# A gated mix of multi-query attention and a state-space convolution: the last softmax normalisation on TensorE, the skip term moved to the end, wide copies for the masters, and four merged stores

## The chip, the cores and the metric

The kernel runs on one core of a Trainium2 chip. The metric is the device time of one execution in microseconds; the span of a profile, from first to last instruction, is about 1.8 us shorter than the time of the same run (552.4 against 554.21 us for the profile of the kernel before).

Engines are named as in the profile: PE multiplies matrices (PEld are its weight loads) and leaves the sums in the memory called PSUM, DVE is the vector engine, ACT the scalar engine, POOL is GpSimd, and SPq and ACTq mark DMA transfers issued by SP and by ACT. To evacuate a tile is to copy it out of PSUM.

## The reference

Two branches read the same x (2048 tokens by 448 channels) and are mixed by a gate per token. Cut to what matters:

```python
g = sigmoid((x * gate_w).sum(-1, keepdims=True))
# A: attention, 16 query heads of 28, one key and value head
q = (x @ wq).reshape(B, S, 16, 28);  k = x @ wk;  v = x @ wv
p = softmax(einsum("bhqd,bkd->bhqk", q, k) * 28 ** -0.5)
a = einsum("bhqk,bkd->bhqd", p, v).reshape(B, S, 448) @ wo
# B: diagonal state space model with 256 states per channel, as a causal convolution
K = einsum("dn,dnl,dn->dl", C, exp(dt * A * l), dt * B).real
b = causal_conv(x, K) + x * Dskip
return g * a + (1 - g) * b
```

## The kernel before

One program for all engines is built from a list of operations with priorities (a smaller number goes first). A list scheduler, which knows an estimated duration for each, fixes the order on every engine before the kernel runs. Four streams share the core:

- Attention. 1024 score tiles (matmul of q and k into PSUM), an exponential on ACT over two or three tiles at once, a value matmul that accumulates in one PSUM bank. The keys' ones column makes row 28 of each group of 32 the softmax denominator. After 16 key tiles the sum is normalised, and after four head groups it is projected with `wo`.
- Tables on the DVE. For each of 28 chunks of 16 channels, powers of the discrete state matrix are doubled up from "masters". Kernel generation on PE turns a table into the convolution kernel, which is evacuated and written to DRAM (`KP_scratch`).
- The convolution on PE: for each chunk four groups of 32 matmuls, each group on one 1 MB Toeplitz tile T that a DMA reads from `KP_scratch` into one of four slots. Then a scaling by 1 - g (`cst`), a transposition on PE (`ytr`) and an add into O, which touches every row of O.
- The skip term x * Dskip * (1 - g), and the stores.

The parts that the change and the argument touch, shortened to a sketch (cuts are marked with `...`):

```python
def norm(self, qc, g):                       # normalisation of head group i = 4 * qc + g
    pg.op("dve", tensor_copy(acc[a], psB))                         # sums out of PSUM
    pg.dma(denT[a] <- row 28 of each 32 of acc[a])                 # (1) spread over 128 partitions
    pg.op("dve", reciprocal(denT[a]))
    pg.dma(R_scratch[i] <- denT[a])                                # (2) to DRAM
    pg.dma(rdenB <- R_scratch[i], each row broadcast to 32 partitions)   # (3) four DMAs
    pg.op("dve", tensor_tensor(onT[i], acc[a], rdenB, MULT))
...
def skip(self):                              # early, priority 53; O was loaded with x before
    for i in range(16):
        pg.op("dve", scalar_tensor_tensor(O[i], O[i], 1 - g, Dskip, MULT, MULT))
...
def masters(self, b):                        # for each of 11 powers k of 7 blocks
    ...
    pg.op("dve", tensor_copy(mbf.real, mst.real))                  # 128 fp32 -> bf16
    pg.op("dve", tensor_tensor(mbf.imag_pair, mst.imag twice, sgn, MULT))   # 256, both signs
...
def kgen(self, c): ... pg.op("pe", mm, pr=3)          # kernel generation
def ytr(self, c):  ... pg.op("pe", mm, pr=3.5)        # transposition of the convolution result
def store(self, i): pg.dma(out[128 rows of i] <- O[i])          # i = 0..15, one queue
```

The DRAM arrays, PSUM banks and the schedule are in the full listing.

Of the kernel before, what the change touches and what calls it, by code (L numbers as in the profile page):

```python
# [11 lines left out]
P = 128  # L12
# [41 lines left out]
class Prog:  # L54
# [13 lines left out]
    def op(self, eng, fn, ns, rd=(), wr=(), pr=0, lat=60, lock=None, unlock=None, comm=None, slack=None, mode="full"):  # L68
        o = Op()
        if eng == "dve" and lat == 60:  # L70
            lat = 105
        o.i, o.eng, o.fn, o.ns, o.lat, o.pr = len(self.ops), eng, fn, ns, lat, pr
        o.lock, o.unlock, o.slot, o.ndma = lock, unlock, None, 0
        o.comm, o.mode = comm, mode
        o.slack = slack if slack is not None else (self.SLACK.get(eng, 0.0) if pr >= 2 else 0.0)
        deps = {}
        if comm is not None:
            deps[self.lastw[comm]] = 1
            self.commops.setdefault(comm, []).append(o.i)
        for k in rd:  # L80
            for c in self.commops.get(k, ()):
                deps[c] = 1
            w = self.lastw.get(k)
            if w is not None:
                deps[w] = 1
        for k in wr:
            w = self.lastw.get(k)
            if w is not None:
                deps[w] = 1
            for r in self.readers.get(k, ()):  # L90
                deps.setdefault(r, 0)
        for k in rd:
            self.readers.setdefault(k, []).append(o.i)
        for k in wr:
            self.lastw[k] = o.i
            self.readers[k] = []
        deps.pop(o.i, None)
        o.deps = deps
        self.ops.append(o)
        return o  # L100
# [15 lines left out]
    def schedule(self):  # L116
# [20 lines left out]
        while done < n:  # L137
            best = None
            for e in ENG:
                T = free[e]  # L140
                for i in ready[e]:
# [7 lines left out]
                    if o.comm in comm:  # L149
                        r = max(r, ops[comm[o.comm]].end)  # L150
# [13 lines left out]
            if o.comm is not None:  # L164
                if o.comm in comm:
                    o.deps[comm[o.comm]] = 1
                comm[o.comm] = i
# [127 lines left out]
class Kernel:  # L295
# [10 lines left out]
    def build(self):  # L306
        nc = self.nc
        with self.es:
# [8 lines left out]
            self.oload()  # L317
# [7 lines left out]
    def alloc(self):  # L325
# [24 lines left out]
        self.dskb = sb("dskb", D, BF)  # L350
# [12 lines left out]
        self.LV = 192  # L363
        self.MC = 5 * 192 + 96
# [5 lines left out]
        self.sgn = sb("sgn", 8, F32)  # L370
# [12 lines left out]
    def consts(self):  # L383
# [10 lines left out]
        for c, val in enumerate([-1.0, 1.0, 1.0, -1.0]):  # L394
            pg.op("pool", lambda e, c=c, val=val: e.memset(V(self.sgn, c, 1), val), 60, wr=["sgn"])
# [18 lines left out]
    def loads(self):  # L414
# [33 lines left out]
        pg.dma([(self.dskb.v(0, P, 0, [[1, D]]), dram(ins["B_Dskip"], 0, [[0, P], [1, D]]))], (128, 896), "dsk", wr=["dsk"])  # L448
# [7 lines left out]
    def oload(self):  # L456
        pg = self.pg
        x = self.ins["A_x"]
        pg.dma([(self.O.v(0, P, 0, [[D, 16], [1, D]]), dram(x, 0, [[D, P], [P * D, 16], [1, D]]))],
               (2048, 896), "ox", rd=[("kT", 3)], wr=["O"], pr=4)  # L460

    def skip(self):
        pg = self.pg
        for i in range(16):
            ov = self.O.v(0, P, D * i, [[1, D]])
            pg.op("dve", lambda e, ov=ov, i=i: e.scalar_tensor_tensor(ov, ov, self.gtok.v(0, P, 16 + i, [[1, 1]]),
                                                                      self.dskb.v(0, P, 0, [[1, D]]), ALU.mult, ALU.mult),
                  el(D), rd=["gt", "dsk", "O"], wr=[("o", i)], pr=53)
        pg.op("dve", lambda e: e.tensor_copy(self.gb.v(0, P, 0, [[1, 16]]), self.gtok.v(0, P, 16, [[1, 16]])), 90,
              rd=["gt"] + [("o", i) for i in range(16)], wr=["O"], pr=53)  # L470
# [5 lines left out]
    def uload(self):  # L476
        pg, x = self.pg, self.ins["A_x"]
        pg.dma([(bass.AP(tensor=self.U.h, offset=16 * D, ap=[[2 * self.U.rs, 64], [1024, 7], [1, 1024]]),
                 dram(self.Z, 0, [[0, 64], [0, 7], [1, 1024]]))], (448, 2048), "uz", rd=["pad", "sw"], wr=["U"], pr=2)
        rs = self.U.rs  # L480
# [87 lines left out]
    def seeds(self):  # L568
# [30 lines left out]
        for s in range(2):  # L599
            o = s * 8192 + 4096 + 31 * 4  # L600
            w = [("tab", s, 0)] + [("xst", k) for k in range(4)] + [("raw", k) for k in range(5)]
            for comp in range(2):
                pg.op("dve", lambda e, o=o, comp=comp: e.memset(self.tab.v(0, P, o + 128 * comp, [[256, 8], [1, 4]]), 1.0 - comp), 80, wr=w, pr=1.5)
# [86 lines left out]
    def masters(self, b):  # L690
# [4 lines left out]
        mo = (b % 2) * self.BC * MC  # L695
        pr = 51.5 + c0 if b else 1.4
# [12 lines left out]
        def src3(k, comp):  # L709
            base = self.seedz if k == 0 else mst  # L710
            off = comp * W2 + B0 if k == 0 else (k % 2) * 2 * BW + comp * BW
            return base.v(0, P, off, [[HC, BC], [1, HC]])

        def src4(k):
            base = self.seedz if k == 0 else mst
            off = W2 + B0 if k == 0 else (k % 2) * 2 * BW + BW
            return base.v(0, P, off, [[4, 8 * BC], [0, 2], [1, 4]])
        for k in range(11):
            ks = "sz" if k == 0 else ("ms", k % 2)
            if k < 5:  # L720
                ro, io, sg = k * 192, k * 192 + 64, 0
            elif k == 5:
                ro, io, sg = 5 * 192, 5 * 192 + 32, 0
            else:
                ro, io, sg = (k - 6) * 192 + 32, (k - 6) * 192 + 128, 2
            lk = ("mb", b % 2, k)
            if k:
# [10 lines left out]
            pg.op("dve", lambda e, k=k, ro=ro: e.tensor_copy(mbf.v(0, P, mo + ro, [[MC, BC], [1, HC]]), src3(k, 0)),  # L738
                  el(BW, 1.92), rd=kk, wr=[lk], pr=pr)
            pg.op("dve", lambda e, k=k, io=io, sg=sg: e.tensor_tensor(  # L740
                mbf.v(0, P, mo + io, [[MC, BC], [1, 64]]), src4(k),
                self.sgn.v(0, P, sg, [[0, 8 * BC], [1, 2], [0, 4]]), ALU.mult),
                el(2 * BW), rd=kk + ["sgn"], wr=[(lk, 1)], pr=pr)

    def tables(self, c):
# [3 lines left out]
        qp = to + 4096  # L749
        b = max(i for i, (c0, n) in enumerate(self.blocks) if c0 <= c)  # L750
        ci = c - self.blocks[b][0]
        mo = (b % 2) * self.BC * self.MC + ci * self.MC
# [4 lines left out]
        pg.op("dve", lambda e: e.tensor_copy(tab.v(0, P, qp + 2048 + 31 * 4, [[256, 8], [128, 2], [1, 4]]),  # L757
                                             self.seedw.v(0, P, c * HC, [[4, 8], [W2, 2], [1, 4]])),
              110, rd=["sw"], wr=[("tab", s, 0)], pr=pr)
        for lv in range(5):  # L760
            w = 1 << lv
            m = mo + lv * 192
# [3 lines left out]
            so_, do_ = qp + (32 - w) * 4, qp + (32 - 2 * w) * 4  # L766
            src = tab.v(0, P, so_, [[128, 32], [1, 4 * w]])
            dst = tab.v(0, P, do_, [[128, 32], [1, 4 * w]])
            pg.op("dve", lambda e, d=dst, a=src, m=m, w=w: e.tensor_tensor(  # L769
                d, a, mbf.v(0, P, m, [[4, 16], [0, 2 * w], [1, 4]]), ALU.mult),  # L770
                el(n, 1.92), rd=rk + mk, wr=[("tab", s, lv + 1)], pr=pr)
            pg.op("dve", lambda e, a=src, m=m, w=w: e.tensor_tensor(  # L772
                tmp.v(0, P, so, [[4 * w, 32], [1, 4 * w]]), a,
                mbf.v(0, P, m + 64, [[4, 32], [0, w], [1, 4]]), ALU.mult),
                el(n, 1.92), rd=rk + mk, wr=[("tmp", s)], pr=pr)
            d2 = tab.v(0, P, do_, [[256, 16], [128, 2], [1, 4 * w]])
            t2 = tmp.v(0, P, so + 4 * w, [[8 * w, 16], [-4 * w, 2], [1, 4 * w]])
            pg.op("dve", lambda e, d=d2, t=t2: e.tensor_tensor(d, d, t, ALU.add), el(n, 1.92),  # L778
                  rd=[("tmp", s), ("tab", s, lv + 1)], wr=[("tab", s, lv + 1)], pr=pr)
        m = mo + 5 * 192  # L780
        mk = [("mb", b % 2, 5), (("mb", b % 2, 5), 1)]
        rk = [("tab", s, l) for l in range(6)]
        src = tab.v(0, P, qp, [[1, 2048]])
        ua = tab.v(0, P, to, [[1, 2048]])
        ub = tab.v(0, P, to + 2048 + 128, [[256, 8], [-128, 2], [1, 128]])
        pg.op("dve", lambda e: e.tensor_tensor(ua, src, mbf.v(0, P, m, [[4, 8], [0, 64], [1, 4]]), ALU.mult),  # L786
              el(2048, 1.92), rd=rk + mk, wr=[("tab", s, 6)], pr=pr)
        pg.op("dve", lambda e: e.tensor_tensor(ub, src, mbf.v(0, P, m + 32, [[4, 16], [0, 32], [1, 4]]), ALU.mult),  # L788
              el(2048, 1.92), rd=rk + mk, wr=[("tab", s, 7)], pr=pr)

    def kgen(self, c):
# [3 lines left out]
        qp = to + 4096  # L795
        tab = self.tab
        X = ("kx", c)
        for jj, comp in ((jj, comp) for jj in range(4) for comp in range(2)):
            def mm(e, jj=jj, comp=comp):
                for half in range(2):  # L800
                    for g in range(4):
                        o = (4 * half + g) * 256 + comp * 128 + jj
                        r = e.matmul(  # L803
                            self.psX.v(32 * g, 32, 96 * jj, [[1, 96]]),
                            tab.v(0, P, qp + 2048 + o, [[4, 32]]), tab.v(0, P, to + o, [[2048, 3], [4, 32]]),
# [3 lines left out]
            pg.op("pe", mm, 165, rd=[("tab", s, l) for l in range(8)], wr=[X, ("kst", c % 2)], pr=3, mode="c32",  # L809
# [23 lines left out]
    def ytr(self, c):  # L833
# [4 lines left out]
        def mm(e):  # L838
            for k in range(4):
# [7 lines left out]
        pg.op("pe", mm, 375, rd=[("cst", cs), "id"], wr=[X], pr=3.5, lock="X", mode="c64")  # L847
        ov = self.O.v(0, P, 15 * D + 16 * c, [[-D, 16], [1, 16]])
        pg.op("dve", lambda e: e.tensor_tensor(ov, ov, self.psX.v(0, P, 0, [[1, 16], [16, 16]]), ALU.add),  # L849
              el(256), rd=[X], comm="O", pr=2, unlock="X")  # L850
# [27 lines left out]
    def outp(self, qc, tt, bank):  # L878
# [3 lines left out]
        lock = "X" if bank == 7 else None  # L882
        kb = [] if bank == 7 else [("b", bank)]
        for g in range(4):
            pg.op("pe", lambda e, g=g: e.matmul(t.v(0, P, o, [[1, D]]), self.onT.v(0, P, ((4 * qc + g) % 6) * 512 + 128 * tt, [[1, 128]]),  # L885
                                                self.Wo.v(0, P, g * D, [[1, D]]), start=(g == 0), stop=(g == 3),
                                                tile_position=(0, 0), skip_group_check=True), 190,
                  rd=["Wo"] + [("on", (4 * qc + k) % 6) for k in range(4)], wr=[X] + kb, pr=2, lock=lock if g == 0 else None)
# [3 lines left out]
              el(D), rd=[X, "gt"] + kb, comm="O", pr=2, unlock=lock)  # L892

    def store(self, i):
        self.pg.dma([(dram(self.out, i * P * D, [[D, P], [1, D]]), self.O.v(0, P, D * i, [[1, D]]))],
                    (128, 896), f"out{i}", rd=["O"], pr=1)

    def norm(self, qc, g):
        pg = self.pg
        i = qc * 4 + g  # L900
        a = i % 2
# [4 lines left out]
        far = 0 if i == 15 else 5000  # L906
# [11 lines left out]
    def main(self):  # L918
# [46 lines left out]
        self.skip()  # L965
# [43 lines left out]
        while c < NCH + LAG:  # L1009
            chunk_step(c)  # L1010
            c += 1
        for tt in range(4):
            self.outp(3, tt, tt)
        for i in range(16):
            self.store(i)
# [48 lines left out]
```

## Time and profile before

| | before |
|---|---|
| time, median | 555.26 us (552.48 to 558.66, 4 runs) |
| span of the profile | 552.4 us |
| last exponential ends | 514.4 us |
| last kernel evacuation starts | 502.7 us |
| last projection add ends | 540.9 us |
| last convolution add ends | 542.9 us |

### The profile page before, as it was taken

To read this page: it belongs to the slowest core of one execution; us is meant where nothing else is said; L and a number is where in the kernel's file an instruction comes from. 1 tells how busy PE (TensorE), PEld (TensorE's weight loads), DVE (VectorE), ACT (ScalarE), POOL (GpSimd) and SP (SyncE) were. 2 spreads that over 40 slices of the span, in tenths; PEclk is the share of its full clock that TensorE was granted. 3 is DMA by queue.
4 is the path that set the end of the run, shared out by engine and by line. 5 is a ranking of instruction groups with operands and counts; after the bars stand their busy time and mean duration, and the time that the engine had idled before them with its cause. 6 is when DMAs were issued, how large, how long until landed. Compare 5 with 4: busy or idle time off the path is not lost.

```text
span 552.4 us, 18386 instructions
## 1 busy us (share of the span) xinstructions
PE 483.9 (88%) x8213; PEld 243.9 (44%) x8213; DVE 489.1 (89%) x1146; ACT 486.7 (88%) x428; POOL 4.7 (1%) x19
## 2 busy tenths in 40 slices
PE   6768978998998999999999999898999999899652
PEld 5411122453544434545455354454554455445421
DVE  3978999999999999999999999999999999991211
ACT  4599999999999999999999999999999999999200
POOL 3000000000000000000000000000000000000000
PEclk9765565999999999999999999999999999989957
DMA  8905408488587378878967786779988798778934
GB/s 227 222 2 133 135 26 305 168 299 332 176 305 289 108 291 298 311 266 305 310 222 257 269 283 199 281 273 369 309 266 316 263 321 309 248 263 288 363 150 133
DMA packets 42014, 136.60 MB, mean 247 GB/s; under 512 B 8684, under 2 KB 24992, under 8 KB 27600
## 3 DMA queue, kind: packets, MB, share of 16 engines
q1 hardware_dynamic: 41200, 135.07, 71.0%
q8 instruction: 64, 1.05, 0.7%
q10 hardware_dynamic: 736, 0.37, 0.3%
q14 instruction: 14, 0.11, 0.1%
HBM read 131.43 MB, written 3.86 MB: 245 GB/s over the span
## 4 chain that ended last, share of the span: by engine, by line
PE 40%; DVE 30%; ACT 21%; DMA 5%; POOL 1%; issue 1%; SPq 0%; POOLq 0%
ACT expT L948 20%; PE psS L938 12%; PE psS L864 10%; PE psB L956 7%; DVE tmp L772 5%; DVE tab L769 5%; DVE tab L778 4%; PE psX L803 4%; DMA T<-KP_scratch 3%; DVE tab L786 2%; PE psX L885 2%; DVE tab L788 2%; DMA R_scratch<-denT 2%; DVE mbf L740 1%; PE psX L678 1%; PE psS L506 1%
## 5 line engine op out<-in xcount | busy, mean ns | idle before, releaser
L948 ACT ACTIVATE expT<-psS 128x1536 bf16<-128x1536 f32 (+1 forms) x410 | 470.0, 1252 | 14.2 <-PE psB L956 9.6
L938 PE MATMUL psS<-qT,kT 29*128 29x512 bf16 x1024 | 172.2, 416 | 34.0 <-ACT expT L948 32.2
L864 PE MATMUL psS<-T,U 128*32 128x128 bf16 (+7 forms) x3584 | 157.4, 303 | 7.2 <-DMA T<-KP_scratch 7.2
L864 PEld LDWEIGHTS psS<-T,U 128*32 128x32 bf16 (+7 forms) x3584 | 113.5, 152 | 39.8 <-issue 24.7
L956 PE MATMUL psB<-expT,vaug 128*32 128x512 bf16 x1024 | 109.7, 419 | 2.4 <-ACT gtok L645 1.4
L938 PEld LDWEIGHTS psS<-qT,kT 29*128 29x128 bf16 x1024 | 39.6, 92 | 130.5 <-ACT expT L948 101.4
L769 DVE TENSOR_TENSOR tab<-tab,mbf 128x1024 bf16<-128x1024 bf16 (+4 forms) x140 | 79.2, 568 | 0.4
L778 DVE TENSOR_TENSOR tab<-tab,tmp 128x1024 bf16<-128x1024 bf16 (+4 forms) x140 | 79.1, 569 | 0.5
L772 DVE TENSOR_TENSOR tmp<-tab,mbf 128x1024 bf16<-128x1024 bf16 (+4 forms) x140 | 79.2, 569 | 0.0
L803 PE MATMUL psX<-tab 128*32 128x96 bf16 x1792 | 58.3, 269 | 1.0 <-DVE O L849 0.8
L956 PEld LDWEIGHTS psB<-expT,vaug 128*32 128x32 bf16 x1024 | 26.7, 95 | 66.6 <-issue 62.2
L803 PEld LDWEIGHTS psX<-tab 128*32 128x32 bf16 x1792 | 43.9, 116 | 12.4 <-issue 6.0
L786 DVE TENSOR_TENSOR tab<-tab,mbf 128x2048 bf16<-128x2048 bf16 x28 | 34.2, 1222 | 0.0
L788 DVE TENSOR_TENSOR tab<-tab,mbf 128x2048 bf16<-128x2048 bf16 x28 | 34.1, 1219 | 0.0
L872 DVE TENSOR_TENSOR cst<-psS,omq 128x512 bf16<-128x512 f32 x28 | 19.2, 685 | 13.9 <-PE psS L864 13.9
L740 DVE TENSOR_TENSOR mbf<-mst,sgn 128x256 bf16<-128x256 f32 x70 | 29.6, 423 | 0.0
L728 DVE TENSOR_TENSOR msq<-mst 128x256 f32<-128x256 f32 x63 | 26.6, 422 | 0.0
L678 PE MATMUL psX<-xT,Wq 112*128 112x512 bf16 x64 | 21.2, 428 | 0.9 <-DVE kstg L818 0.8
L731 DVE TENSOR_TENSOR mst<-msq 128x128 f32<-128x128 f32 x70 | 20.2, 289 | 0.0
L915 DVE TENSOR_TENSOR onT<-acc,rdenB 128x512 bf16<-128x512 f32 x16 | 11.0, 688 | 9.9 <-DMA rdenB<-R_scratch 9.9
L734 DVE SCALAR_TENSOR_TENSOR mst<-mst 128x128 f32<-128x128 f32 x63 | 18.3, 290 | 0.0
L738 DVE CAST mbf<-mst 128x128 bf16<-128x128 f32 x70 | 15.8, 225 | 0.0
(103 smaller groups left out, 248.6 us busy)
## 6 DMA issues: line engine op xcount, KB each, us to landing
T<-KP_scratch SPq DMA_DIRECT2D x112, 1024.0 KB, 8.0
rdenB<-R_scratch SPq DMA_DIRECT2D x64, 64.0 KB, 4.1
U<-in_A_x_dram SPq DMA_DIRECT2D x3, 896.0 KB, 5.4
tab<-in_A_x_dram SPq DMA_DIRECT2D x4, 448.0 KB, 6.9
O<-in_A_x_dram SPq DMA_DIRECT2D x1, 1792.0 KB, 9.9
KP_scratch<-kstg SPq DMA_DIRECT2D x28, 64.0 KB
out_dram<-O SPq DMA_DIRECT2D x16, 112.0 KB, 1.8
U<-Z_scratch SPq DMA_DIRECT2D x1, 896.0 KB, 7.9
```

The lines of the kernel that those rows point to most:

```text
L678: pg.op("pe", lambda e, T=T: e.matmul(px, self.Wq.v(0, DT, T * 512 + g * 128, [[1, 128]]), self.xT.v(0, DT, T * S + 512 * qc, [[1, 512]]), ...
L740: pg.op("dve", lambda e, k=k, io=io, sg=sg: e.tensor_tensor(mbf.v(0, P, mo + io, [[MC, BC], [1, 64]]), src4(k), self.sgn.v(0, P, sg, [[0, ...
L769: pg.op("dve", lambda e, d=dst, a=src, m=m, w=w: e.tensor_tensor(d, a, mbf.v(0, P, m, [[4, 16], [0, 2 * w], [1, 4]]), ALU.mult), el(n, 1.9 ...
L772: pg.op("dve", lambda e, a=src, m=m, w=w: e.tensor_tensor(tmp.v(0, P, so, [[4 * w, 32], [1, 4 * w]]), a, mbf.v(0, P, m + 64, [[4, 32], [0, ...
L778: pg.op("dve", lambda e, d=d2, t=t2: e.tensor_tensor(d, d, t, ALU.add), el(n, 1.92), rd=[("tmp", s), ("tab", s, lv + 1)], wr=[("tab", s, l ...
L786: pg.op("dve", lambda e: e.tensor_tensor(ua, src, mbf.v(0, P, m, [[4, 8], [0, 64], [1, 4]]), ALU.mult), el(2048, 1.92), rd=rk + mk, wr=[(" ...
L788: pg.op("dve", lambda e: e.tensor_tensor(ub, src, mbf.v(0, P, m + 32, [[4, 16], [0, 32], [1, 4]]), ALU.mult), el(2048, 1.92), rd=rk + mk, ...
L803: r = e.matmul(self.psX.v(32 * g, 32, 96 * jj, [[1, 96]]), tab.v(0, P, qp + 2048 + o, [[4, 32]]), tab.v(0, P, to + o, [[2048, 3], [4, 32]] ...
L864: r = e.matmul(ps.v(32 * j, 33 - m, po + 128 * k, [[1, 128]]), self.U.v(0, P, (m - 1) * D + 4 * gi + j, [[D, 33 - m]]), self.T.v(0, P, s * ...
L938: r = e.matmul(self.psS.v(0, P, 1536 * s + 512 * k, [[1, 512]]), kT.v(32 * h, DH + 1, 128 * kt, [[1, 128]]), qT.v(32 * h, DH + 1, 512 * qs ...
L948: pg.op("act", lambda e: e.activation(expT.v(0, P, 512 * (i0 % 10), [[1, n]]), self.psS.v(0, P, 1536 * s, [[1, n]]), AF.Exp, scale=SQ), 75 ...
L956: r = e.matmul(self.psB.v(32 * h, 32, 0, [[1, 512]]), vaug.v(0, P, 32 * kt, [[1, 32]]), expT.v(0, P, 512 * ((4 * st + h) % 10), [[1, 512]] ...
```

## The change

The intent is to shorten the tail behind the last exponential and to take work off the DVE. Cut to its core:

```diff
 def norm(self, qc, g):
+    if i == 15: return self.norm_last(i)
+def norm_last(self, i):                      # no DMA
+    fid = fp32 identity                        # in the dead seedz space
+    for tt in range(4): acc[tt] <- psB[tt]             # DVE, 128 columns each
+    for tt in range(4): psB[4*tt:] = acc[tt].T @ fid[:, 28::32]   # fp32 matmul
+    denT = reciprocal(psB[:16]);  rde = denT spread to 512 columns          # DVE
+    for tt in range(4): bank4[tt] = rde[tt].T @ fid      # fp32 matmul
+    for tt in range(4): onT[tt] = acc[tt] * bank4[tt]    # DVE
 ...
-    x loaded into O at the start; skip() early: O[i] = O[i] * (1-g) * Dskip          (pr 53)
+    O zeroed by a DMA at the start; skip() recorded last, x reloaded into dead xT:
+        xT[i] = xT[i] * (1-g) * Dskip ;  O[i] += xT[i]                               (pr 90)
 ...
-    tensor_copy(mbf.real, mst.real)            # 128
-    tensor_tensor(mbf.imag_pair, mst.imag twice, sgn, MULT)         # 256
+    tensor_copy(mbf.real and mbf.imag, mst both)         # 256
+    tensor_scalar(mbf.neg_imag, mst.imag, -1.0, MULT)    # 128
     ... layout of mbf and of the tables changed to suit
 ...
-    kgen pr=3,  ytr pr=3.5
+    kgen pr=1.9, ytr pr=1.8
 ...
-    store(i) for 16 tiles, one queue, each waiting for all of O
+    store(qc) for 4 quarters, two queues, each waiting for its quarter of O
```

The first three of the four matmuls of each last projection tile also stop waiting for the last head group, and the scheduler's slack for the head group before the last becomes 2000 ns instead of 5000.

## The prediction

> **What bounds the kernel now.** I read the busy times in stretches first, then the order of time of the end, then the chain of work that ended last, and the DMA issues. The stretches (columns: window, its length, then busy time and count for PE, weight load, DVE, ACT and GpSimd, then granted clock, DMA share and GB/s) divide the 552.4 us span:
>
> ```profile
> 24.00:42.00 18.00, 13.55 (x139) 5.59 (x137) 14.81 (x31) 16.88 (x16) 0.00 (x0) 0.59 0.08 23
> 200.00:300.00 100.00, 94.53 (x1784) 50.17 (x1785) 99.47 (x236) 97.47 (x86) 0.00 (x0) 0.98 0.79 278
> 300.00:400.00 100.00, 94.65 (x1723) 48.61 (x1718) 99.84 (x242) 98.21 (x87) 0.00 (x0) 1.00 0.79 281
> 503.00:514.50 11.50, 9.54 (x167) 4.51 (x165) 1.48 (x4) 11.13 (x11) 0.00 (x0) 1.00 0.90 290
> 514.50:534.00 19.50, 9.91 (x264) 7.58 (x264) 3.29 (x7) 0.00 (x0) 0.00 (x0) 0.70 0.80 302
> 534.00:543.00 9.00, 7.07 (x60) 3.31 (x60) 4.33 (x7) 0.00 (x0) 0.00 (x0) 0.70 0.00 0
> 543.00:552.40 9.40, 0.00 (x0) 0.00 (x0) 0.00 (x0) 0.00 (x0) 0.00 (x0) 0.68 0.60 195
> ```
>
> The reader is to see two kernels in one. From about 42 to 514.5 us ACT does exponentials 97 to 98% of the time; the DVE is just as full but finishes its tables near 503. The exponentials set the end of that phase, and no part of the change removes one. From 514.5 us ACT is idle and 38 us follow in which no engine is full. That tail is what can be shortened. In order of time it reads:
>
> ```profile
> 514.89 0.69 DVE L904 COPY acc<-psB 128x512 f32<-128x512 f32 x1 [0.73 <-PE psB L956]
> 515.61 0.59 SPq L106 DMA_DIRECT2D denT<-acc  x1
> 519.69 0.59 SPq L106 DMA_DIRECT2D R_scratch<-denT  x1
> 529.31 2.74 SPq L106 DMA_DIRECT2D rdenB<-R_scratch  x4
> 531.89 0.18 PEld L864 LDWEIGHTS psS<-T,U 128*32 128x32 bf16 x4 [1.84 <-DMA T<-KP_scratch]
> 533.79 0.69 DVE L915 TENSOR_TENSOR onT<-acc,rdenB 128x512 bf16<-128x512 f32 x1 [9.86 <-DMA rdenB<-R_scratch]
> 534.54 5.62 PE L885 MATMUL psS<-Wo,onT 128*128 128x448 bf16 x16 [2.28 <-DVE onT L915]
> 540.26 0.68 DVE L891 SCALAR_TENSOR_TENSOR O<-psS,gtok,O 128x448 bf16<-128x448 f32 x1 [0.27 <-PE psS L885]
> 542.45 0.42 DVE L849 TENSOR_TENSOR O<-O,psX 128x256 bf16<-128x256 bf16 x1 [0.54 <-PE psX L842]
> 542.89 7.70 SPq L106 DMA_DIRECT2D out_dram<-O  x16
> ```
>
> The last normalisation takes 514.89 to 533.79 us, nearly all of it three DMA steps. The chain of waits puts 9.60 us on one of them, the write of 8 KB to scratch:
>
> ```profile
> 510.10 7.74 DMA T<-KP_scratch
> 519.69 9.60 DMA R_scratch<-denT
> 531.62 2.15 DMA rdenB<-R_scratch
> ```
>
> That write was issued behind three 1 MB loads of T (issued from 516.30), whose convolution groups start at 517.88, 520.81, 524.14, 526.62, 529.12 and 531.89. So a second chain runs in the same tail: the last eight convolution groups (256 of the 3584 matmuls of that line fall after 514.5), one load each every 2.5 to 3.3 us. It would have ended near 533 without the output projection put into the last group (4 of its matmuls before, 28 after).
>
> **What the Trainium skill says.** "DMA: Bandwidth & Descriptors", section "Queues, rings and completion order", has descriptors of one engine's ring consumed in ring order; the 9.60 us of the small write behind the T loads agree. The same page, "Issuing engines are not separate DMA queues", says that issuing on several engines saves only sequencer time; this bears on the stores, where sixteen issues take 7.70 us of sequencer. "VectorE: DVE Perf Modes", section "Mode 2×_2P — use both read ports for one tensor", lets fp32 copies and tensor-scalar operations in SBUF run at two elements a cycle, while a tensor-tensor operation on fp32 cannot. The trace agrees (starts, duration):
>
> ```profile
> 441.14 0.22 DVE L738 CAST mbf<-mst 128x128 bf16<-128x128 f32 x1
> 441.28 0.42 DVE L740 TENSOR_TENSOR mbf<-mst,sgn 128x256 bf16<-128x256 f32 x1
> 441.61 0.42 DVE L728 TENSOR_TENSOR msq<-mst 128x256 f32<-128x256 f32 x1
> ```
>
> The next start comes 0.14 us after the cast of 128 and 0.33 us after the multiply of 256; durations overlap, so I count start to start. "FP8 and Floating Point Precision" (its note on true FP32) gives four passes through the array for an fp32 matmul; this trace has none to check it.
>
> **The change, part by part.**
>
> Normalisation. Three DMA steps go. In their place, after the last value matmul at 514.85 us: four 128-column copies from PSUM (128-element PSUM reads last 0.28 us and follow each other after 0.20): 0.9. Four fp32 matmuls that transpose four denominator columns: loading four passes of 128 weights at 0.15 us, as the output projection's weight loads take here, is 0.6 each, less some overlap: 2. Reciprocal 0.25. A 512-element copy that spreads it, two a cycle: 0.4. Four fp32 matmuls of 128 columns, the same loads plus four passes of 128 columns at the tail's clock: 2.5. Four multiplies from PSUM: first after 0.3, last after 0.9. Waits between engines, 0.05 to 0.1 each: 0.4. That is near 522 instead of 534.5. The first three of each tile's four projection matmuls no longer wait for it, so twelve of the sixteen, 0.35 us each, run meanwhile; four remain, then four DVE adds at 0.6 us: the attention chain ends near 524.2, where it ended at 540.9. Gain 16.7 us if nothing else holds the end.
>
> DVE work. Masters: per step, a cast of 128 (0.14) and a multiply of 256 (0.33) become a copy of 256 at two a cycle (0.20) and a scale of 128 (0.14). Saved 0.13, times 77 steps: 10 us. Runs of four bf16 elements in the destination should not lower the rate: the tables with runs of four already take only 0.22 us for 128. Skip: sixteen operations, 0.60 us apart, leave the stretch 47.8 to 77 us (9.6 us freed at the start); they return after the last query projection (422.8 us) with sixteen bf16 adds of 0.30: 14.4 us. The scheduler starts whatever is ready first, so I expect them soon after the reload of x, in front of the last tables. Net on the last table: -10 - 9.6 + 14.4 = -5 us; -20 if the skip goes behind the tables. The new table layout keeps counts and types: 0.
>
> Kernel-generation matmuls, now of higher priority: the last table ends at 496.55, but their result is evacuated at 502.74, because they were filled in between other PE work over 498.4 to 502.5. Gain here 2 to 4 us. Together the last convolution moves 5 to 10 us earlier, from 533 to 523 to 528, and ends with its evacuation, transposition and add (1.9 us) near 527.
>
> Stores. Before: 542.87 to 552.4, 9.5 us, paced by sixteen issues of 0.48. The DMA share of 0.60 over 9.4 us says the transfers need 5.6. Four issues, two on each of two queues, leave 0.5 to 1 of issue, 5.6 of transfer and about 1.2 of landing (the small stores land 1.8 us after issue): 7.5. Saved 2. All four wait for the last convolution's add, which writes all rows; only if that is done first is just the last quarter left, about 3.5 us.
>
> Sum: the later of 524.2 and 527, plus 7.5, is 534.5. I add 1 us for a disturbed exponential phase, and 1.8 for what the measured time of the profiled run (554.21) has over its span: 537, taken as 536 since either chain may be last. Against 554.4 this is -3.3%.
>
> **Rivals.**
>
> 1. The convolution takes the place of the normalisation. For it: T loads at 0.80 DMA share already fill the tail, and the reload of x, 1.8 MB in one go (such a load took 9.9 us to land at the start), pushes into the same ring late. If the last add stays at 535, the end is 535 + 7.5 + 1.8 = 544.5: a gain just under 2%. Against it: the freed DVE time and the 6 us between the last table and its evacuation.
>
> 2. Everything clears the tail: the skip runs behind the tables, the last group is done by 514 to 520, and only the attention chain and the last quarter of the stores remain: 524.2 + 3.5 + 1.8 = 529.5. For it: PE has 5% idle in the main phase, and eight groups are just 9.8 us of PE work. Against it: T loads come at about 3.3 us each near the end, so a backlog of eleven groups after 503 cannot vanish with 5 us.
>
> 3. The exponential phase gets longer. Kernel generation and convolution transposes move in front of other PE work and below the priority from which the scheduler leaves 500 ns of slack; if DVE is late, PE stands still, in order. ACT's idle time before exponentials is only 14.2 us in the whole run, so it is easily made worse: some 3 to 6 us. Against it: these waits overlap a double-buffered score bank. This would give 539 to 542.
>
> 4. The fp32 matmuls cost twice my estimate: +4 us on the attention chain, 528, still mostly hidden beside the convolution: +1.
>
> **Range and chances.** Rival 2 sets the low end, 528; rival 1 with some of rival 3 the high end, 545. Faster by over 2% means under 543.3. The normalisation gain is large and certain, and rival 1 alone only just misses; I give 0.85. Within 2%: 0.14. Slower by over 2% would need the main phase 20 us longer: 0.01.
>
> **What would show it.** Right: exponentials still end at 513 to 517; from there to the first projection add 7 to 9 us with no DMA between; the scratch writes are fifteen; masters' new copy lasts about 0.29 us, the scale about 0.22; skip operations lie between 425 and 500; the last kernel evacuation lies at 492 to 500; stores take 7 to 8 us. Wrong: the copy of 256 at 0.42 (the mode lost), convolution groups still waiting on T after 527, exponentials ending after 518, or stores past 9 us.

## More of the kernel before

From the page: the busy line, then groups (line, engine, operation, output and inputs, shapes, count; busy time and mean nanoseconds; idle time of the engine just before them, and what ended most of it).

```profile
PE 483.9 (88%) x8213; PEld 243.9 (44%) x8213; DVE 489.1 (89%) x1146; ACT 486.7 (88%) x428; POOL 4.7 (1%) x19
...
L948 ACT ACTIVATE expT<-psS 128x1536 bf16<-128x1536 f32 (+1 forms) x410 | 470.0, 1252 | 14.2 <-PE psB L956 9.6
...
L864 PE MATMUL psS<-T,U 128*32 128x128 bf16 (+7 forms) x3584 | 157.4, 303 | 7.2 <-DMA T<-KP_scratch 7.2
...
L740 DVE TENSOR_TENSOR mbf<-mst,sgn 128x256 bf16<-128x256 f32 x70 | 29.6, 423 | 0.0
```

Three engines stand at 88 or 89%, which tells nothing by itself. Convolution matmuls (L864) waited 7.2 us for T, and nearly all of that is in the tail (six waits there add up to 7.05).

## The result, and the profile after

The changed kernel took 538.48 us median (536.9 to 539.63, 4 runs) beside 555.26 for the kernel before. The ratio is 0.9693, with a 95% interval of 0.9631 to 0.9755. A later job gave 539.55 against 554.52 us, ratio 0.9734 (0.9692 to 0.9775). Ratios here are the mean time of one kernel's fast runs over that of the other's of the same rounds, so not quite the ratio of the medians.

| | before | changed |
|---|---|---|
| span of the profile | 552.4 | 537.2 |
| last kernel evacuation starts | 502.7 | 491.2 |
| last exponential ends | 514.4 | 519.5 |
| last projection add ends | 540.9 | 529.2 |
| last convolution add ends | 542.9 | 529.8 |
| from there to the end | 9.5 | 7.4 |

The page of the changed kernel, with the lines that answer to those of before. L977 is the exponential, L853 the convolution, L727 and L730 the two new operations of the masters:

```profile
PE 484.8 (90%) x8229; PEld 243.8 (45%) x8229; DVE 483.9 (90%) x1168; ACT 487.5 (91%) x428; POOL 4.9 (1%) x17
...
L977 ACT ACTIVATE expT<-psS 128x1536 bf16<-128x1536 f32 (+1 forms) x410 | 470.8, 1254 | 19.0 <-PE psB L985 12.9
...
L853 PE MATMUL psS<-T,U 128*26 128x128 bf16 (+7 forms) x3584 | 157.9, 303 | 0.6 <-DMA T<-KP_scratch 0.5
...
L727 DVE CAST mbf<-mst 128x256 bf16<-128x256 f32 x70 | 20.1, 288 | 0.1
...
L730 DVE TENSOR_SCALAR mbf<-mst 128x128 bf16<-128x128 f32 x70 | 15.3, 218 | 0.0
```

Busy times hardly moved. What moved is in the last columns: the convolution's wait for T fell from 7.2 to 0.5 us, and ACT's idle time before exponentials rose from 14.2 to 19.0 us. The stretches of the tail (window, length, then PE, weight loads, DVE, ACT and GpSimd busy, granted clock, DMA share, GB/s):

```profile
503.00:514.50 11.50, 9.86 (x169) 5.04 (x169) 1.11 (x2) 11.50 (x12) 0.00 (x0) 1.00 1.01 343
514.50:519.55 5.05, 4.58 (x78) 2.37 (x78) 0.69 (x1) 5.03 (x5) 0.00 (x0) 1.00 0.70 237
519.55:529.80 10.25, 8.72 (x115) 5.47 (x115) 6.66 (x16) 0.00 (x0) 0.00 (x0) 1.00 0.01 2
529.80:537.20 7.40, 0.00 (x0) 0.00 (x0) 0.00 (x0) 0.00 (x0) 0.00 (x0) 0.59 0.77 248
```

The DMA share is the thing to see: after the last exponential it is 0.01, where before it was 0.80. All T loads have landed by then, so PE is 85% busy and at full clock instead of waiting. The order of time from the last value matmul (start, duration; x8 for four fp32 matmuls):

```profile
519.58 0.40 PE L985 MATMUL psB<-expT,vaug 128*32 128x512 bf16 x4
520.03 1.27 DVE L899 COPY acc<-psB 128x128 f32<-128x128 f32 x4 [4.69 <-PE psB L985]
521.35 1.06 PE L906 MATMUL psB<-seedz,acc 128*128 128x4 f32 x8
523.40 1.16 PE L915 MATMUL psS<-seedz 128*128 128x128 f32 x8
524.60 1.25 DVE L920 TENSOR_TENSOR onT<-acc,psS 128x128 bf16<-128x128 f32 x4 [1.43 <-PE psS L915]
526.77 1.08 PE L853 MATMUL psS<-T,U 128*30 128x128 bf16 x28
528.55 0.68 DVE L883 SCALAR_TENSOR_TENSOR O<-psS,gtok,O 128x448 bf16<-128x448 f32 x1
529.33 0.42 DVE L838 TENSOR_TENSOR O<-O,psX 128x256 bf16<-128x256 bf16 x1
529.78 1.05 ACTq L106 DMA_DIRECT2D out_dram<-O  x2
```

From the last exponential to the last projection add is now 9.7 us (519.5 to 529.2), where it was 26.5. But the last two convolution groups are run in pieces between the matmuls of the normalisation and of the projection, from 523.12 to 527.85 (the last piece is L853 at 526.77), and the add of the last comes after everything else. No store can start before it.

### The profile page after: what moved, and what is told of

Read it like the earlier page. It is cut to its first block, busy times and chain, and to the rows that moved or that the text cites. A ratio compares the mean times of both kernels' runs of the same rounds, so it can differ in the third digit from the quotient of the medians.

```text
span 537.2 us, 18418 instructions
## 1 busy us (share of the span) xinstructions
PE 484.8 (90%) x8229; PEld 243.8 (45%) x8229; DVE 483.9 (90%) x1168; ACT 487.5 (91%) x428; POOL 4.9 (1%) x17
## 4 chain that ended last, share of the span: by engine, by line
PE 47%; ACT 36%; DVE 12%; DMA 2%; issue 1%; POOL 1%; DVEq 0%; POOLq 0%
ACT expT L977 35%; PE psS L967 13%; PE psS L853 12%; PE psB L985 8%; PE psX L792 6%; PE psX L676 2%; DMA T<-KP_scratch 2%; DVE tab L767 2%; DVE tmp L762 2%; DVE tab L759 2%; PE psS L504 1%; PE psX L877 1%; PE psX L831 1%; DVE O L883 1%; DVE tab L776 1%
## 5 line engine op out<-in xcount | busy, mean ns | idle before, releaser
L977 ACT ACTIVATE expT<-psS 128x1536 bf16<-128x1536 f32 (+1 forms) x410 | 470.8, 1254 | 19.0 <-PE psB L985 12.9
L853 PE MATMUL psS<-T,U 128*26 128x128 bf16 (+7 forms) x3584 | 157.9, 303 | 0.6 <-DMA T<-KP_scratch 0.5
L853 PEld LDWEIGHTS psS<-T,U 128*26 128x26 bf16 (+7 forms) x3584 | 113.9, 152 | 35.3 <-issue 28.2
L762 DVE TENSOR_TENSOR tmp<-tab,mbf 128x2048 bf16<-128x2048 bf16 (+4 forms) x140 | 78.0, 563 | 0.0
L759 DVE TENSOR_TENSOR tab<-tab,mbf 128x2048 bf16<-128x2048 bf16 (+4 forms) x140 | 77.9, 563 | 0.0
L767 DVE TENSOR_TENSOR tab<-tab,tmp 128x2048 bf16<-128x2048 bf16 (+4 forms) x140 | 77.8, 563 | 0.0
L792 PE MATMUL psX<-tab 128*32 128x96 bf16 x1792 | 54.8, 268 | 1.3 <-issue 1.2
L792 PEld LDWEIGHTS psX<-tab 128*32 128x32 bf16 x1792 | 41.2, 116 | 14.2 <-issue 9.0
L727 DVE CAST mbf<-mst 128x256 bf16<-128x256 f32 x70 | 20.1, 288 | 0.1
L804 DVE TENSOR_REDUCE kstg<-psX 128x128 bf16<-128x256 f32 x28 | 11.7, 418 | 4.2 <-PE psX L792 4.1
L730 DVE TENSOR_SCALAR mbf<-mst 128x128 bf16<-128x128 f32 x70 | 15.3, 218 | 0.0
```

Of the source, the lines that this page charges most:

```text
L759: pg.op("dve", lambda e, d=dst, a=src, ra=ra, w=w: e.tensor_tensor(d, a, mbf.v(0, P, ra, [[8, 16], [0, 2 * w], [1, 4]]), ALU.mult), el(n, ...
L762: pg.op("dve", lambda e, a=src, rb=rb, w=w: e.tensor_tensor(tmp.v(0, P, so, [[4 * w, 32], [1, 4 * w]]), a, mbf.v(0, P, rb, [[4, 32], [0, w ...
L767: pg.op("dve", lambda e, d=dst, t=t2: e.tensor_tensor(d, d, t, ALU.add), el(n, 1.92), rd=[("tmp", s), ("tab", s, lv + 1)], wr=[("tab", s, ...
L792: r = e.matmul(self.psX.v(32 * g, 32, 96 * jj, [[1, 96]]), tab.v(0, P, o + 768, [[4, 32]]), tab.v(0, P, o, [[256, 3], [4, 32]]), start=(co ...
L853: r = e.matmul(ps.v(32 * j, 33 - m, po + 128 * k, [[1, 128]]), self.U.v(0, P, (m - 1) * D + 4 * gi + j, [[D, 33 - m]]), self.T.v(0, P, s * ...
L977: pg.op("act", lambda e: e.activation(expT.v(0, P, 512 * (i0 % 10), [[1, n]]), self.psS.v(0, P, 1536 * s, [[1, n]]), AF.Exp, scale=SQ), 75 ...
```

## The experiments

The total was as predicted. The question was whether it came the way the prediction said. Twelve kernels ran. Those called "undo" take one part out of the changed kernel, those called "alone" put one part into the kernel before. Each was also profiled, and the times of events below are from that one profile, so they carry the scatter of single runs (1.2 us between the two profiles of the changed kernel).

| run | time, us | ratio to before (95%) | exponentials end | last projection add | last convolution add | span |
|---|---|---|---|---|---|---|
| changed, second job | 539.55 | 0.9734 (0.9692 to 0.9775) | 518.3 | 527.9 | 528.5 | 535.9 |
| undo normalisation | 535.61 | 0.9663 (0.9596 to 0.9729) | 518.1 | 530.5 | 524.5 | 533.7 |
| undo skip | 536.77 | 0.9676 (0.9639 to 0.9713) | 514.8 | 524.2 | 525.9 | 533.4 |
| undo both | 536.40 | 0.9660 (0.9624 to 0.9696) | 515.3 | 529.8 | 523.0 | 533.1 |
| undo masters | 539.73 | 0.9729 (0.9702 to 0.9756) | 520.0 | 529.3 | 532.1 | 539.6 |
| undo stores | 541.24 | 0.9746 (0.9716 to 0.9776) | 519.9 | 529.6 | 530.1 | 539.7 |
| undo priorities | 542.10 | 0.9784 (0.9731 to 0.9837) | 516.5 | 527.6 | 532.7 | 540.1 |
| normalisation alone | 549.52 | 0.9915 (0.986 to 0.9969) | 514.3 | 525.5 | 537.2 | 546.8 |
| priorities alone | 548.61 | 0.9912 (0.9843 to 0.998) | 515.5 | 538.6 | 532.8 | 548.1 |
| masters alone | 545.09 | 0.9818 (0.9778 to 0.9859) | 516.4 | 535.1 | 526.5 | 544.7 |
| last convolution first | 538.20 | 0.9687 (0.9651 to 0.9723) | 523.2 | 533.7 | 530.7 | 538.2 |

**Undo normalisation.** The last head group goes through DRAM again; that the first three projection matmuls of each tile don't wait for it is kept:

```diff
-        if i == 15:
-            return self.norm_last(i)
-        far = 5000 if i < 14 else 2000
+        far = 0 if i == 15 else 5000 if i < 14 else 2000
-            rd = [("onl", tt) if g == 3 else on[g]] if last else on
+            rd = [on[g]] if last else on
```

> The changed kernel with the last normalisation sent through DRAM again, all else as changed. Theory A (the three DMA steps are slow because the T loads fill the ring, and the last normalisation carries most of the gain): the scratch write is again stuck for some 9 us, the projection starts 18 to 20 us after the last exponential, and the time is 549 to 554 us. Rival (the ring is emptier in the changed kernel, where the T loads come earlier, so the DMA way is cheap by itself): from the last exponential to the projection 10 to 12 us, time 541 to 546 us, the gain over before still 1.5 to 2.5%.

Measured: 535.61 us, better than either theory and no slower than the changed kernel. This is the run that overturned the prediction's account. The chain of waits of this kernel, at the three DMA steps:

```profile
519.28 1.88 DMA denT<-acc
521.47 1.49 DMA R_scratch<-denT
524.25 2.00 DMA rdenB<-R_scratch
```

And its last issues of T before them:

```profile
508.55 3.06 SPq L106 DMA_DIRECT2D T<-KP_scratch  x2
```

The scratch write that took 9.60 us before takes 1.49. The whole way from the copy of the sums (518.56) to the start of the multiply (526.27) is 7.7 us, where it was 18.9. The three steps are those of the kernel before. What differs is the T loads ahead of them in the ring (the queue in which issued transfers wait): here the last was issued by 511.6, well before the first step at 519.28; before, four more were issued from 516.30 on, around these steps. From the last exponential to the last projection add the DMA way takes 12.4 us and the PE way 9.7. Yet while the DMA way waits, PE and DVE are free, the convolution is done at 524.5, and the stores of three quarters are issued then. After the last projection add only one quarter is left: 3.2 us instead of 7.4.

**Normalisation alone.** The same part put into the kernel before.

```diff
+        if i == 15:
+            return self.norm_last(i)
```

> The kernel before with only the last normalisation through PE. Theory A (the convolution takes the normalisation's place): projection adds done 10 us after the last exponential, near 525, but the last convolution group still waits for T until 530 or later, its add lies at 532 to 536, and the time is 544 to 549 us. Rival (the normalisation alone is the whole gain): time 536 to 540 us.

Measured: 549.52 us, just above the range of theory A; the rival (536 to 540) falls. The projection adds are done at 525.5, 15 us earlier than before, and the convolution takes their place. One line of its chain of waits says it:

```profile
525.39 8.68 DMA T<-KP_scratch
```

After that wait comes the last group, and its add ends at 537.2, a little past the 532 to 536 expected.

**Undo priorities, and priorities alone.** The edit of the first; the second is the reverse of it, in the kernel before.

```diff
-            pg.op("pe", mm, 165, ..., pr=1.9, mode="c32", ...)      # kgen
+            pg.op("pe", mm, 165, ..., pr=3, mode="c32", ...)
-        pg.op("pe", mm, 375, ..., pr=1.8, lock="X", mode="c64")     # ytr
+        pg.op("pe", mm, 375, ..., pr=3.5, lock="X", mode="c64")
```

> The changed kernel with the old priorities of kernel generation and convolution transposes (3 and 3.5). In the changed kernel the last exponential ends at 519.5 us against 514.4 before. Theory A (convolution work that lay in the tail now fills PE in the main phase and delays value matmuls): the end of the exponentials stays at 517 to 521, time 537 to 542 us. Rival B (the new priorities, without slack, make PE stand): the exponentials end at 513 to 515.5 and the time falls to 532 to 535 us.

> The kernel before with only the new priorities. Rival B: the exponentials end at 518 or later and the time rises by 3 to 6 us, to 557 to 561 us. Theory A: the exponentials end within 2 us of 514.4, the last kernel evacuation comes 2 to 5 us earlier, and as the normalisation still goes through DRAM the time is 551 to 556 us.

Undone, the time rises to 542.10 us. The exponentials end at 516.5, between the two theories' ranges, so they don't decide; the fall to 532 to 535 us of rival B did not come. What costs is that the last group again waits 6.1 us for its T load, to 529.7. Alone, they bring 548.61 us, below both ranges. The exponentials end 1.1 us later than before, so rival B (518 or later) falls. The last evacuation comes only 1.0 us earlier (501.8), less than theory A said, but the last convolution add ends at 532.8, and the scratch write falls from 9.6 to 5.5 us. The whole way from the copy of the sums (516.02) to the multiply (531.79) falls less, from 18.9 to 15.8 us, since the first DMA step now takes 5.74 us; two T loads were still issued behind it, from 517.37.

**Undo skip.** The reload of x and the late adds go; O is loaded with x and scaled early. Dskip is kept in the space of log dt, since there is no room left for it.

```diff
-    O zeroed by a DMA; skip() after the last chunk, x reloaded into xT (pr=90)
+    oload() at the start; skip() before masters(0), in place in O (pr=53)
+    dskb = self.dt32
```

> The changed kernel with the skip term done early again: x loaded into O at the start, sixteen multiplies near 47 to 80 us, no reload of x and no late adds. Theory A (DVE time decides when the last kernel evacuation comes; in the changed kernel it is at 491 to 492 us against 502.7 before, and the late skip costs 4.8 us of DVE more than the early one): the last evacuation moves to 485 to 489 us, the convolution has no wait for T, and the time is 534 to 539 us, no worse than with the change. Rival C (the early 9.6 us are what bring the convolution forward, since work at the start delays all chunks and the late skip falls into gaps): the last evacuation moves back to 496 to 502 us, the last groups wait for T again, and the time is 542 to 547 us.

Measured: 536.77 us, as theory A said: the last evacuation starts at 488.4, 2.8 us earlier than in the changed kernel. The unexpected part is the exponentials, which end at 514.8.

**Undo masters.** Old operations, old table layout.

```diff
-            tensor_copy 256 fp32 -> bf16 (real and imag);  tensor_scalar 128 * -1.0
+            tensor_copy 128 fp32 -> bf16 (real);  tensor_tensor 256 * sgn
```

> The changed kernel with the old masters (cast of 128 and sign multiply of 256) and the old table layout. Theory A: 10 us of DVE come back, the last kernel evacuation lies at 499 to 503 us, the last convolution groups wait for T to 528 or later, time 543 to 548 us. Rival (the masters fill gaps of the DVE and cost the end nothing): last evacuation still at 490 to 494 us, time 537 to 540 us.

Measured: 539.73 us, in the rival's range. The DVE part of theory A holds (the last evacuation starts at 502.2), the time does not follow: by the ratios, 10 us on the DVE cost 0 to 0.4% here. The convolution runs without a break on PE from the projection to 530.4, so here PE's order sets its end and no longer T.

**Masters alone.** The same part put into the kernel before.

```diff
-            tensor_copy 128 fp32 -> bf16 (real);  tensor_tensor 256 * sgn
+            tensor_copy 256 fp32 -> bf16 (real and imag);  tensor_scalar 128 * -1.0
-    dskb a buffer of its own
+    dskb = self.dt32
```

> The kernel before with only the new masters and the new table layout (Dskip is kept in the space of log dt to make room). Theory A' (DVE time moves the convolution, and an earlier convolution by itself unblocks the DMA normalisation): last kernel evacuation at 491 to 496 us instead of 502.7, the scratch write of the last normalisation takes 2 to 6 us instead of 9.6, time 543 to 550 us. Rival (the convolution's place in PE order does not follow): evacuation early but the scratch write still near 9 us and the time within 0.6% of before.

Measured: 545.09 us, the largest gain of the three parts tried alone, and in each number as theory A' said: last evacuation at 491.1, scratch write 2.2 us.

```profile
517.64 4.25 DMA denT<-acc
522.19 2.22 DMA R_scratch<-denT
```

With not one instruction of the normalisation changed, its way from the copy of the sums (516.93) to the multiply (527.70) shrank from 18.9 to 10.8 us: the convolution is done at 526.5, before the projection, and the T loads are out of the ring sooner. After the last projection add the old sixteen stores follow.

**Undo stores.**

```diff
-        pg.dma([(4 tiles)], ..., f"out{qc}", ..., eng="act" if qc % 2 else "sp")
+        for i in range(4 * qc, 4 * qc + 4):
+            pg.dma([(1 tile)], ..., f"out{i}", ...)
```

> The changed kernel with sixteen stores of 112 KB on one queue instead of four on two. Theory A (issue of 0.48 us each paces them): the stores take 9.0 to 9.7 us after the last add instead of 7.4, time up by about 2 us to 540 to 541.5 us. Rival (the transfer of 1.8 MB paces them anyway): within 0.7 us of the changed kernel, 537.5 to 539.5 us.

Measured: 541.24 us. From the last add to the end is 9.6 us (530.1 to 539.7) instead of 7.4: the issues pace them, as theory A said.

**Last convolution first.** An attempt to get the early stores with the PE normalisation.

```diff
-    convolution of chunk 27: pr=2.5, its scaling and add pr=2, its ytr pr=1.8
+    convolution of chunk 27, its scaling, ytr and add: pr=-2
```

> The changed kernel with the last chunk's convolution, its transposition and its adds put ahead of everything else. In the run without the PE normalisation the convolution was done at 524.5 us, three of the four stores ran early, and the end came 3.3 us after the last projection add. Theory D (with the PE normalisation the last group is squeezed in between its matmuls, so that all four stores start at 529.8): now the last convolution add comes by 526 us, at most two stores remain after the last projection add, and the time is 532 to 536 us. Rival (the last group is held by its T load, which is issued at 512.5 us, or the normalisation is pushed back by as much): last convolution add at 527 to 530 us or the last projection add at 531 or later, time 537 to 540 us.

Measured: 538.20 us, the rival's range. The adds come no earlier (530.7), and the exponentials end at 523.2. The timeline shows the price: a full group stands in front of a value matmul whose tiles ACT needs back.

```profile
521.21 1.94 ACT L977 ACTIVATE expT<-psS 128x1536 bf16<-128x1536 f32 x2 [1.37 <-PE psB L985]
```

**Undo both, and the changed kernel again**. The first has the edits of undo normalisation and undo skip, the second none.

> The changed kernel with both the early skip and the normalisation through DRAM, so that only masters, table layout, priorities and merged stores are left of the change. Theory A' (early convolution empties the ring of T loads before the last exponential; then the DMA normalisation takes 8 us and leaves PE to the convolution, and the early skip keeps the exponentials at 515): exponentials end at 514.5 to 517, last convolution add at 520 to 523, last projection add 12.4 us after the exponentials, end 3.3 us later, time 531 to 535 us, better than the changed kernel by 0.5 to 1.2%. Rival (each of these was run-to-run scatter of 1 to 2 us): within 0.4% of the changed kernel of the same job.

> The changed kernel again, unchanged but for a comment, as the yardstick of this job: 537 to 540 us, exponentials ending at 518 to 520.5 in its profile. If they end at 515 to 517, the 5 us by which they ended later is mostly scatter from run to run.

Measured: 536.40 against 539.55 us by median, five rounds each. What is left in the first, that is masters, table layout, priorities and merged stores, has the whole gain of the change (0.9660), and without the two parts that head the description it is 0.6% faster; its time is above the range that I gave, the difference inside. Its exponentials end at 515.3, its last convolution add at 523.0, its last projection add 14.5 us after the exponentials (12.4 expected: the way through DRAM, 516.07 to 525.61, took 9.5 us here and not 7.7). It and the kernels with the normalisation or the skip alone undone are the fastest here (0.9660, 0.9663, 0.9676), and the three cannot be told apart. With the skip early, the normalisation through PE (undo skip, 536.77 us) or through DRAM (536.40 us) makes no difference either. The changed kernel's exponentials end at 518.3 in this second profile, so their lateness is not just scatter.

**A quarter of the convolution.** Wrong in its result on purpose, a single look, so of state unknown.

```diff
-            for m in range(1, 16, 2):
+            for m in (1, 15):
```

> The changed kernel with a quarter of the convolution matmuls (8 of 32 in each group, same T loads), wrong in its result on purpose: takes 118 us of PE work away. Theory E (PE, 95% busy, sets the gaps between exponentials, so convolution work moved out of the tail costs them time): the exponentials end at 505 to 511 us. Rival (the gaps come from waits on DVE or from the scheduled order): they end at 516 to 520 us as in the changed kernel.

Measured: 563.46 us, with the exponentials ending at 538.8. Neither theory gave this. The same stretch in the changed kernel and in this one (granted clock is the third number from the right):

```profile
200.00:300.00 100.00, 95.47 (x1865) 51.29 (x1865) 98.69 (x242) 97.27 (x86) 0.00 (x0) 1.00 0.81 287
```

```profile
200.00:300.00 100.00, 89.22 (x1110) 31.72 (x1110) 91.92 (x216) 90.64 (x79) 0.00 (x0) 0.70 0.72 248
```

There are 755 fewer matmuls in the stretch, and the clock is 0.70 instead of 1.00; over the whole run, a median score matmul takes 0.601 us instead of 0.385. The PE time saved was mostly given back as slower matmuls, so the run can't say what the removed work cost. That the missing matmuls lowered the clock is likely but not shown by one execution of unknown state. It is inconclusive for its question.

## Why the prediction was right, and where its account was not

**The time.** 536 was predicted, 528 to 545 as the range; 538.48 and 539.55 us were measured. The sum holds, in part by luck: two of its terms are off in opposite directions. The exponentials ended 5.1 us later, where 1 was allowed; from their end to the last convolution add it took 10.3 us, where 12.6 was forecast (527 less 514.4). And the reason given as "large and certain" is not the cause. Two slips in its working change nothing: rival 1 adds up to 544.3, not 544.5, and the DVE's last table ends at 496.55, not near 503, where the last evacuation is.

**The step that failed: the normalisation's gain.** The prediction said that it "is large and certain", 16.7 us on the attention chain. Its local numbers are near: 9.8 us from the exponentials to the last projection add predicted, 9.7 measured; the first of these adds came after 6.4 us, a little sooner than the 7 to 9 named as a sign of being right. The fp32 matmuls were over-estimated (2 and 2.5 us; 1.06 and 1.16 measured), and waits behind other work made up for it: from the last multiply to the last projection add took 3.4 us instead of 2.0. What failed is the comparison. It was made against the DMA way as the kernel before shows it, 18.9 us, of which 9.6 belonged to T loads in the ring. The prediction read that correctly, and even named the write as stuck "behind three 1 MB loads of T", but did not ask what the DMA way would cost once the other parts of the same change had moved those loads: 7.7 us. So the local gain is 2.7 us (12.4 less 9.7), and it is given back because the last convolution groups wait among the matmuls of the normalisation and the projection and hold all four stores: 7.4 us follow the last add, where 3.2 follow without it. This last is read from the two traces; the run meant to test it (last convolution first) did not bring the convolution forward. With it and without, the changed kernel takes the same time within what these runs can tell (0.9693 and 0.9734 with, 0.9663 without, the intervals overlapping).

**Rival 1, in part.** That the convolution takes the normalisation's place is what the kernel with the normalisation alone does: 0.9915. In the whole change it happens in a milder form: the two chains end within 0.6 us of each other, at 529.2 and 529.8.

**DVE work and evacuation.** The new copy was expected at 0.29 and the scale at 0.22 us: 0.288 and 0.218. The last evacuation was to lie at 492 to 500 and starts at 491.2. The late skip operations run from 445.0 to 495.5 us, in front of the last tables, as predicted. The busy time of the masters' two operations fell from 45.4 to 35.4 us, the 10 us predicted. Here the account is right, and here most of the gain can be had: masters alone 1.8%, priorities alone 0.9%, and with the merged stores, without normalisation and late skip, the whole of it. Added alone, both let the convolution finish earlier, and with that the old normalisation got faster (10.8 and 15.8 us instead of 18.9 from copy to multiply). But the gain isn't theirs alone: the normalisation alone brings 0.9% too, and undoing the masters costs only 0 to 0.4%.

**The exponential phase, rival 3.** Allowed for with 1 us; it came out at +5.1 in the first profile and +3.9 in the second, past the 518 that the prediction named as a sign of error. It took the priorities to be the cause. The priorities alone add 1.1 us. The late skip is the better candidate. In the five profiles with it and the new priorities (the changed kernel twice, and with the normalisation, the masters or the stores undone) the exponentials end at 518.1 to 520.0; in the two with the early skip and the new priorities, at 514.8 and 515.3. With the late skip and the old priorities it is 516.5, so the two may act together. How it does so is open. In those five profiles no late operation runs before 444 us, and yet ACT has lost time by then: between 42 and 444 us it is busy 386.4 to 387.9 us, and 389.3 and 389.6 in the two with the early skip and the new priorities (391.9 before). So the larger part of the loss can't come from those operations standing in the way. It may come from the order that the scheduler finds without them at the start, or from the load of PE; this is not shown, and the run meant to separate the two failed by the clock.

**Stores.** 7.5 us predicted, 7.4 measured; sixteen again 9.6. The expected 2 us are there in the tail; the ratios say 0.1 to 0.5%, too near their intervals to say more.

**Parts do not add up.** Undoing one part at a time costs at most 0.9% each, and for two of them nothing, while the whole is worth 2.7 to 3.1%. Three chains end close together, so each part alone mostly hands the end to another chain. A rival for the small differences stays untested: each edit makes the scheduler order everything anew, and no run here shows what a change of order without meaning is worth. Differences of half a per cent are not to be put down to one part.

## What to carry to other kernels

A slow small DMA in a profile may be slow only because of what is ahead of it in its ring; before replacing it, ask what it will cost after the other parts of the change have emptied that ring. When several chains race to one end, judge a part by undoing it in the final kernel as well as by adding it to the first, since the two answers can differ (for the normalisation 0.9% added to the first, nothing in the final one). And a replacement that is faster by itself can gain nothing if it uses the engines that the slower one left free for the last work.

## What the Trainium skill lacked or had wrong

- "FP8 and Floating Point Precision", the note on true FP32: it gives four passes, from which I estimated four fp32 matmuls at 2 to 2.5 us. The trace records each as two matmuls and two weight loads (whether a record holds two passes can't be seen), and four of them took 1.06 us with 4 columns and 1.16 us with 128, so the columns hardly mattered. What the page lacks is how many weight loads an fp32 matmul takes and what they cost: here eight of them took 0.97 us.
- "TensorE: Matmul & The Clock Gate", section "What's actually happening": it gives a window of time for the release of the throttle, but no share of busy time within it that holds the clock. The runs show that the share read from a profile doesn't tell: with a quarter of the convolution PE was busy 86 to 89% of the stretches between 100 and 400 us and was granted 0.70 to 0.77 (a single execution of unknown state; its span was 24.5 us longer than the changed kernel's, with 2688 fewer matmuls), while in the changed kernel 85 to 86% (503.00 to 514.50 and 519.55 to 529.80) had 1.00. What decides is open.
